# Weight-conversion halves of a fused attention and gated-layer kernel paced by 0.24 instead of 0.38 a unit, up to unit 21 instead of 24

## The chip, the cores and the metric

The kernel runs on one core of a Trainium2 chip. The metric is the device time of one execution in microseconds (us), as the median of several executions. A difference of over 0.2% (2.0 us here) is told apart from no change.

## What is computed

Causal attention with a decay (batch 4, 8 heads, 576 positions, head size 64), then a gated layer (512 to 1536 to 512), then a second layer (512 to 2048 to 512), all over 2304 tokens:

```
scores = scale * (q @ k^T) + cum[i] - cum[j], causal; attn = softmax(scores); x = attn @ v
x = (sigmoid(x @ w_gate) * (x @ w_val)) @ w_out
h = x @ w_in;  x = (h * clip(h + 3, 0, 6) / 6) @ w_out2
```

The five weights arrive as 64-bit floats and are used as pairs of 32-bit numbers (a high part and a rest).

## The kernel before

**Attention.** The 32 heads are taken as 16 pairs. Each pair has four **units** (row blocks of queries), so there are 64 units, numbered by `t`; pairs 0 to 6 take them in rising order, later pairs in falling order. For unit `t`, PE (TensorE) first turns the probabilities of unit `t - 3` (`tt`, L220; three units deep), then computes the scores of unit `t` (`st`, L216). DVE (VectorE) adds the decay and finds the row extreme (L500, two to four instructions a unit), ACT (ScalarE) takes the exponential (L508), DVE forms the reciprocal (L543, L544), POOL (GpSimd) normalises (L546). Scores have three PSUM banks and a unit uses two, so the scores of unit `t + 1` wait until the first L500 of unit `t` has read its bank. At the last unit of a pair PE also forms probabilities times values (`pv <- etA, etB`). Up to pair 6 PE turns q and k (`tq`, `tk`, `tl`, with DVE copies such as L415 and L426); from pair 7 on DVE turns them (L398, L399, L402).

**Filler.** From unit 23 on, one group of 12 matmuls of the gated layer is put into most units by `Filler.one` (L779): for each of three token chunks of 512, eight groups `pg` and `pv` (gate and value, four each) and then four groups `po` (output). The last unit of a pair has none. A group is only begun when its weights have been issued (`Gated.after`, L699); if they haven't, the unit goes without a group. Groups that are left when the attention ends run behind it, back to back.

**Conversion.** The weights of these groups are made in 12 **halves** (two each for gate 0, value 0, gate 1, value 1, output 0, output 1). A half loads 512 KB, takes three DVE instructions on 128x512 (L107, L108, L114) with one ACT instruction (L111) between the second and the third, then a high part (POOL L64 for halves issued before unit 16, ACT L62 from there on) and a rest (POOL L65). `Converter.run(n, engs)` (L183) adds `n` to an account at each unit from unit 4 on and issues a half for each full 1.0. A scheduler then places the instructions on each engine; each engine runs its own in that order.

Of the kernel before, what the change touches and what calls it, by code (L numbers as in the profile page):

```python
# [20 lines left out]
def attn_moe_kernel(  # L21
# [21 lines left out]
    NQ = 4  # L43
# [150 lines left out]
    conv = Converter()  # L194
# [856 lines left out]
    class Second:  # L1051
# [93 lines left out]
        def unit(self, k, x, ys, temps, between={}):  # L1145
            u1, u2, p5 = temps
            g, tt = self.ga[k % 2], nc.vector.tensor_tensor
            r11, r22, r12 = self.act(u1, g, 0, 0), self.act(p5, g, 1, 1), self.act(u2, g, 1, 0)
            r21 = self.act(x(), g, 0, 1)
            then = {1: (r11,), 2: (r11,), 3: (r11,), 4: (r22,), 5: (r12, r22, r22), 6: (r21, r12, r12, r21, r21)}  # L1150
            for s in range(7):
                if s in (1, 3):
                    y = ys.pop(0)()
                o = y if s % 2 else x()
                self.product(o, k, s, s in (0, 1, 3))
                if s in (0, 2, 3):
                    nc.scalar.copy({0: u1, 2: u2, 3: p5}[s], o)  # L1157
                elif s < 6:
                    c = {1: u1, 4: p5, 5: u2}[s]
                    tt(c, c, o, ALU.add)  # L1160
                for r in then.get(s, ()):
                    next(r)
                if k % NQ2 == NQ2 - 1:
                    self.load_block(k // NQ2 * 7 + 7 + s)
                if s in between:
                    between[s]()
# [72 lines left out]
    EA = (nc.scalar, nc.gpsimd, nc.gpsimd)  # L1239
    EF = (nc.scalar, nc.scalar, nc.gpsimd)  # L1240
    WU = (8, 4, 4, 4)

    KD, KT, RT = 4, 7, 0

    CA, C0, CB, CC = 0.65, 4, (1.8, 1.0, 1.5, 1.7, 2.0), 1.0

    CE, CS = 0.38, 0.12


    NGA, NCA, GA = 2, 3, 1  # L1250

    NSA = 8
# [111 lines left out]
    for t in range(len(units) + 3):  # L1364
        for job in (fixed, expo, norm, prep):
            job(t)
        if t == 2:
            eight = ep.tile([P, S], F32, tag="e", name="eight")[: B * H]
            nc.vector.tensor_scalar(eight, cum, -8.0, 1.0, ALU.mult, ALU.mult)
            nc.sync.dma_start(cum_d[1], eight)  # L1370
        p, s = unit(t - 4)
        if p and s == p.order[-1] and p.hp == NP - 1 and p.b < NCA:
            done = p.b + 1
        p, s = unit(t - 5)
        if p and s == p.order[-1] and t < len(units) + 3:
            fill.load(p.b, p.hp + 1)
        if t >= C0:
            conv.run(CS if len(conv.jobs) <= 2 * NSA - 6 * NGA else CE if t < NQ * (KT - 1) else CA, EA if t < NQ * KD else EF)
        fill.n = done
    att.close()  # L1380
    pace["dve"] = None
# [63 lines left out]
```

## Time and profile before

| what | value |
|---|---|
| median of 3 runs | 1002.28 us (1002.18 to 1002.36) |
| profiled execution, its own time | 1003.57 us |
| its span, first to last instruction | 1001.8 us |
| busy share of PE, DVE, ACT, POOL over the span | 98%, 53%, 48%, 29% |
| granted TensorE clock, mean | 0.998 of full speed |

The span is 1.77 us shorter than the profiled execution's own time, and that execution is 1.29 us above the median of the runs. Times inside the profile count from the start of the span. The attention ends at about 279 us; the two layers fill the rest.

### The profile page before, as it was taken

The numbers are of one execution on the slowest core, as the hardware profiler recorded it, in microseconds if no ns is written. First come the engines' busy times: TensorE is split into PE (matmuls) and PEld (weight loads), VectorE is DVE, ScalarE is ACT, GpSimd is POOL, SyncE is SP. The second block draws the span as 40 slices with busy tenths as digits, with TensorE's granted clock in tenths as the row PEclk, the third lists the DMA queues.
The fourth block names the chain that finished last, engine by engine and source line by source line (L and its number), as shares of the span: only waits on it lengthen the run. The fifth ranks groups of instructions, "written<-read, shape, count | busy, mean of one in ns | idle before, by whom it ended". The sixth has DMA issues, their size and how long they took to land.

```text
span 1001.8 us, 16150 instructions
## 1 busy us (share of the span) xinstructions
PE 986.5 (98%) x5733; PEld 810.4 (81%) x5733; DVE 530.9 (53%) x1220; ACT 476.9 (48%) x1094; POOL 290.5 (29%) x360
## 2 busy tenths in 40 slices
PE   8889999999999999999999999999999999999998
PEld 4556766667688889988888888899899898998987
DVE  6777856645347543737777574553534443333322
ACT  6787677667634432424434343453444443433322
POOL 3675655545323220302334131111111111111110
PEclk9999999999999999999999999999999999999999
DMA  7999796744324352566977578654686845753211
GB/s 184 294 250 226 198 244 156 185 143 145 119 79 154 117 166 82 175 210 264 331 258 252 179 270 318 245 198 166 237 330 206 293 147 193 294 209 148 81 66 64
DMA packets 141072, 197.30 MB, mean 197 GB/s; under 512 B 84192, under 2 KB 93408, under 8 KB 136896
## 3 DMA queue, kind: packets, MB, share of 16 engines
q1 hardware_dynamic: 140944, 196.20, 59.9%
q8 instruction: 45, 0.74, 0.3%
q14 instruction: 35, 0.29, 0.1%
q10 hardware_dynamic: 48, 0.07, 0.0%
HBM read 142.88 MB, written 53.36 MB: 196 GB/s over the span
## 4 chain that ended last, share of the span: by engine, by line
PE 91%; DVE 3%; ACT 2%; DMA 2%; issue 1%; POOL 0%; SPq 0%; DVEq 0%; ACTq 0%; POOLq 0%
PE po L216 34%; PE pv L216 18%; PE u L216 17%; PE pg L216 15%; PE st L216 4%; PE tt L220 3%; DVE e L500 1%; DMA kn<-in_k_dram 1%; ACT e L508 1%; DMA cum_d<-eight 1%; DMA x_d<-x 0%; DVE raw L108 0%; ACT raw L111 0%; ACT etB L580 0%; PE o L216 0%
## 5 line engine op out<-in xcount | busy, mean ns | idle before, releaser
L216 PE MATMUL po<-w,big 128*128 128x512 f32 x864 | 200.5, 390 | 0.0
L216 PEld LDWEIGHTS po<-w,big 128*128 128x128 f32 x864 | 161.8, 188 | 32.8
L216 PE MATMUL pg<-big,wg 128*128 128x512 f32 (+1 forms) x720 | 161.9, 371 | 0.0
L216 PE MATMUL pv<-big,wv 128*128 128x512 f32 (+1 forms) x720 | 161.4, 371 | 0.0
L216 PE MATMUL po<-big,wo 128*128 128x512 f32 (+1 forms) x720 | 160.9, 371 | 0.2 <-DVE big L65 0.2
L216 PEld LDWEIGHTS pg<-big,wg 128*128 128x128 f32 x720 | 125.8, 189 | 27.2 <-issue 4.0
L216 PEld LDWEIGHTS pv<-big,wv 128*128 128x128 f32 x720 | 125.6, 189 | 26.8 <-issue 4.5
L216 PEld LDWEIGHTS po<-big,wo 128*128 128x128 f32 x720 | 125.6, 189 | 25.7 <-issue 2.2
L1160 DVE TENSOR_TENSOR h<-h,u 128x384 f32<-128x384 f32 x69 | 38.2, 554 | 154.0 <-PE u L216 154.0
L546 POOL TENSOR_SCALAR e<-e,m 128x256 f32<-128x256 f32 (+4 forms) x144 | 86.8, 617 | 48.8 <-DVE m L544 32.1
L508 ACT ACTIVATE e<-e,m 128x256 f32<-128x256 f32 (+4 forms) x144 | 83.6, 584 | 31.6 <-DVE m L500 20.3
L216 PE MATMUL u<-h,big 128*128 128x384 f32 x504 | 90.2, 336 | 0.4 <-DVE h L1160 0.4
L216 PE MATMUL u<-h,h 128*128 128x384 f32 x504 | 90.1, 336 | 0.0
L216 PEld LDWEIGHTS u<-h,big 128*128 128x128 f32 x504 | 88.3, 188 | 1.8 <-DVE h L1160 0.8
L216 PEld LDWEIGHTS u<-h,h 128*128 128x128 f32 x504 | 88.4, 188 | 1.0
L1109 POOL TENSOR_TENSOR big<-tail,big 128x384 fp32r<-128x384 f32 x30 | 30.5, 1018 | 196.5 <-PE u L216 115.5
L1157 ACT COPY h<-u 128x384 f32<-128x384 f32 x69 | 32.8, 475 | 111.5 <-PE u L216 111.5
L500 DVE CUSTOM_DVE_ANT_0 e<-st,dc 128x384 f32<-128x384 f32 (+3 forms) x110 | 53.5, 520 | 47.9 <-PE st L216 30.3
L872 DVE SCALAR_TENSOR_TENSOR sg<-sg,pv 128x512 f32<-128x512 f32 (+1 forms) x48 | 29.7, 618 | 92.3 <-PE pv L216 59.7
L111 ACT ACTIVATE raw<-raw 128x512 f32<-128x512 f32 x68 | 45.6, 682 | 67.1 <-DVE raw L108 64.5
L62 ACT CAST big<-sg 128x512 fp32r<-128x512 f32 (+1 forms) x60 | 34.8, 580 | 60.6 <-DVE sg L872 54.6
L114 DVE SCALAR_TENSOR_TENSOR raw<-raw 128x512 int32<-128x512 int32 x68 | 52.5, 782 | 19.4 <-ACT raw L111 18.9
(141 smaller groups left out, 1202.8 us busy)
## 6 DMA issues: line engine op xcount, KB each, us to landing
h<-xc_d SPq DMA_DIRECT2D x21, 768.0 KB, 7.2
big<-x_d SPq DMA_DIRECT2D x28, 512.0 KB, 5.8
raw<-in_moe_w_out_dram SPq DMA_DIRECT2D x28, 512.0 KB, 3.7
h<-wt_d SPq DMA_DIRECT2D x12, 1024.0 KB, 7.4
big<-wt_d SPq DMA_DIRECT2D x12, 1024.0 KB, 7.6
x_d<-x SPq DMA_DIRECT2D x16, 576.0 KB, 3.9
h<-wb_d SPq DMA_DIRECT2D x12, 768.0 KB, 4.6
big<-wb_d SPq DMA_DIRECT2D x12, 768.0 KB, 5.2
```

Of the source, the lines that this page charges most:

```text
L62: nc.scalar.copy(hi, src)
L111: nc.scalar.activation(e, e, AF.Copy, scale=2.0**-112)
L114: nc.vector.scalar_tensor_tensor(low, high, 3, low, ALU.logical_shift_left, ALU.bitwise_or)
L216: i = nc.tensor.matmul(*a, **k)
L220: i = nc.tensor.transpose(*a)
L500: i = nc.vector.tensor_tensor_reduce(out=e, in0=st, in1=d, op0=ALU.add, op1=ALU.min, scale=self.by, scalar=init, accum_out=m[:, a : a + 1],)
L508: nc.scalar.activation(e, e, AF.Exp, bias=m[:, a : a + 1], scale=-1.0, accum_out=m[:, 4 + b : 5 + b])
L546: pace["pool"] = nc.gpsimd.tensor_scalar(e, e, m[:, 12 + j : 13 + j], 1.0, ALU.mult, ALU.mult)
L872: pace["dve"] = nc.vector.scalar_tensor_tensor(sg, sg, 1.0, pv, ALU.add, ALU.mult)
L1109: (nc.vector if f else nc.gpsimd).tensor_tensor(lo, sg, hi.bitcast(F32), ALU.subtract)
L1157: nc.scalar.copy({0: u1, 2: u2, 3: p5}[s], o)
L1160: tt(c, c, o, ALU.add)
```

## The change

The account gets 0.24 instead of 0.38 a unit, and the faster rate of 0.65 begins at unit 21 instead of unit 24 (`NQ * (KT - 1)`). The rate of 0.12 after the twelfth half stays.

```
-    CE, CS = 0.38, 0.12
+    CE, CS, CT = 0.24, 0.12, 21
...
-            conv.run(CS if len(conv.jobs) <= 2 * NSA - 6 * NGA else CE if t < NQ * (KT - 1) else CA, EA if t < NQ * KD else EF)
+            conv.run(CS if len(conv.jobs) <= 2 * NSA - 6 * NGA else CE if t < CT else CA, EA if t < NQ * KD else EF)
```

Worked through the account, the twelve halves are issued at these units:

```
before: 6  9 11 14 17 19 22 24 26 27 29 30
change: 8 12 16 20 22 23 25 27 28 30 31 33
```

On DVE, the first half, before (units 6 to 7 of pair 1; `raw` is the weight, `e` the scores with decay, `x` the attention's output):

```order
L544 RECIPROCAL m<-m 128x2
L107 TENSOR_SCALAR raw<-raw 128x512
L646 TENSOR_TENSOR x<-pv,x 128x256
L108 SCALAR_TENSOR_TENSOR raw<-raw 128x512
L114 SCALAR_TENSOR_TENSOR raw<-raw 128x512
L646 TENSOR_TENSOR x<-pv,x 128x320
L500 ISA e,m<-st,dt 128x288
```

and with the change (units 8 to 9 of pair 2):

```order
L415 TENSOR_SCALAR qp<-tq 128x512
L544 RECIPROCAL m<-m 128x1
L107 TENSOR_SCALAR raw<-raw 128x512
L108 SCALAR_TENSOR_TENSOR raw<-raw 128x512
L500 ISA e,m<-st,dc 128x384
L500 ISA m 128x1
L500 ISA e,m<-st,dc 128x384
L500 ISA m 128x1
L543 TENSOR_SCALAR m<-m 128x4
L426 COPY kp<-tk 128x512
L114 SCALAR_TENSOR_TENSOR raw<-raw 128x512
```

The whole half stood ahead of the last unit's L500 of a pair; now two of its instructions stand ahead of the second unit's L500 and the third behind it. The halves of units 12, 16 and 20 stand at the same place of pairs 3, 4 and 5.

On PE, units 32 to 34 before (`po` is an output group, `wo` its weights):

```order
L216 MATMUL st<-kp,qz_144 128x288 x2
L216 MATMUL po<-big,wo_1692 128x512 x6
L216 MATMUL po<-big,wo_1883 128x512 x6
L220 MATMUL tt<-ident,e 128x64 x12
L216 MATMUL st<-kp,qp 128x512 x2
L216 MATMUL po<-big,wo_1692 128x512 x6
L216 MATMUL po<-big,wo_1883 128x512 x6
L220 MATMUL tt<-ident,e 128x64 x12
L216 MATMUL st<-kp,qp 128x384 x2
```

and with the change:

```order
L216 MATMUL st<-kp,qz_144 128x288 x2
L220 MATMUL tt<-ident,e 128x64 x12
L216 MATMUL st<-kp,qp 128x512 x2
L220 MATMUL tt<-ident,e 128x64 x12
L216 MATMUL st<-kp,qp 128x384 x2
```

The twelfth half now comes at unit 33, so units 32 and 33 have no group; every later group stands two slots later, and three instead of one `po` groups are left for the end of the attention. Up to unit 31 the order on PE is the same in both.

On DVE, between units 31 and 32 before:

```order
L398 STREAM_TRANSPOSE qp<-qn 128x512
L399 STREAM_TRANSPOSE kp<-kn 128x576
L544 RECIPROCAL m<-m 128x2
L726 SCALAR_TENSOR_TENSOR sg<-sg,pv 128x512
L500 ISA e,m<-st,dt 128x288
```

and with the change:

```order
L398 STREAM_TRANSPOSE qp<-qn 128x512
L399 STREAM_TRANSPOSE kp<-kn 128x576
L544 RECIPROCAL m<-m 128x2
L107 TENSOR_SCALAR raw<-raw 128x512
L108 SCALAR_TENSOR_TENSOR raw<-raw 128x512
L726 SCALAR_TENSOR_TENSOR sg<-sg,pv 128x512
L114 SCALAR_TENSOR_TENSOR raw<-raw 128x512
L500 ISA e,m<-st,dt 128x288
```

The half of unit 31 now stands ahead of the first L500 of unit 32.

## Rows read from the trace of the kernel before

**Rows 1.** Page, part 1: busy us, share of the span, instructions.
```profile
PE 986.5 (98%) x5733; PEld 810.4 (81%) x5733; DVE 530.9 (53%) x1220; ACT 476.9 (48%) x1094; POOL 290.5 (29%) x360
```

**Rows 2.** Stretch table: length; busy PE, PEld, DVE, ACT, POOL; clock, DMA share, GB/s.
```profile
36.00:83.00 47.00, 41.27 (x425) 24.86 (x425) 38.10 (x138) 41.17 (x128) 34.80 (x50) 1.00 0.98 267
...
100.00:126.00 26.00, 26.00 (x209) 18.32 (x208) 21.80 (x61) 18.43 (x51) 16.93 (x20) 1.00 0.75 202
```

**Rows 3.** Timeline of PE, units 4 to 23: start, length, instruction, [idle before, releaser].
```profile
18.69 0.50 PE L216 MATMUL st<-masks,identb 128*128 128x384 bf16 x2
...
32.02 0.51 PE L216 MATMUL st<-masks,identb 128*128 128x384 bf16 x2 [2.06 <-DVE m L500]
...
44.46 0.50 PE L216 MATMUL st<-masks,identb 128*128 128x384 bf16 x2
...
48.18 0.29 PE L216 MATMUL st<-masks,identb 128*128 128x128 bf16 x2 [1.41 <-ACT raw L111]
...
58.19 0.50 PE L216 MATMUL st<-masks,identb 128*128 128x384 bf16 x2 [0.70 <-DVE m L500]
...
70.24 0.50 PE L216 MATMUL st<-masks,identb 128*128 128x384 bf16 x2 [0.20 <-DVE m L500]
...
73.64 0.29 PE L216 MATMUL st<-masks,identb 128*128 128x128 bf16 x2 [1.09 <-ACT raw L111]
...
82.95 0.27 PE L220 MATMUL tl<-ident,kn 128*128 128x128 f32 x1
```

**Rows 4.** Stretch table of PE around the idle at 32 us; clock behind the bracket.
```profile
33.00:34.00 1.00, 1.00 (x14) 0.50 1.20 191
...
36.00:37.00 1.00, 1.00 (x20) 1.00 1.01 249
```

**Rows 5.** Timeline of DVE: second unit of pair 2 and of pair 4.
```profile
37.46 0.56 DVE L500 CUSTOM_DVE_ANT_0 e<-st,dc 128x384 f32<-128x384 f32 x1 [0.65 <-PE st L216]
...
62.99 0.56 DVE L500 CUSTOM_DVE_ANT_0 e<-st,dc 128x384 f32<-128x384 f32 x1 [0.96 <-POOL dt L386]
```

**Rows 6.** Groups of DVE by shape, 20 to 83 us: busy us, mean ns, idle before.
```profile
L108 DVE SCALAR_TENSOR_TENSOR raw<-raw 128x512 int32<-128x512 int32 x7 | 5.9, 839 | 0.1
...
L114 DVE SCALAR_TENSOR_TENSOR raw<-raw 128x512 int32<-128x512 int32 x7 | 4.8, 692 | 2.2 <-ACT raw L111 2.2
...
L107 DVE TENSOR_SCALAR raw<-raw 128x512 int32<-128x512 int32 x7 | 2.9, 408 | 0.0
```

**Rows 7.** The same groups of DVE, 100 to 126 us.
```profile
L108 DVE SCALAR_TENSOR_TENSOR raw<-raw 128x512 int32<-128x512 int32 x4 | 3.9, 980 | 0.1
L114 DVE SCALAR_TENSOR_TENSOR raw<-raw 128x512 int32<-128x512 int32 x4 | 3.3, 824 | 1.6 <-ACT raw L111 1.4
L107 DVE TENSOR_SCALAR raw<-raw 128x512 int32<-128x512 int32 x4 | 2.8, 712 | 0.0
```

**Rows 8.** Timeline of PE, units 32 to 35.
```profile
126.03 2.80 PE L216 MATMUL po<-big,wo 128*128 128x512 f32 x10
...
129.74 0.59 PE L220 MATMUL tt<-ident,e 64*128 64x64 f32 x12
130.16 1.08 PE L216 MATMUL st<-kp,qp 64*128 64x512 f32 x4
131.17 3.06 PE L216 MATMUL po<-big,wo 128*128 128x512 f32 x12
134.15 0.58 PE L220 MATMUL tt<-ident,e 64*128 64x64 f32 x12
...
138.59 0.87 PE L216 MATMUL st<-kp,qp 64*128 64x128 f32 x8
```

**Rows 9.** Timeline of DVE between units 31 and 32.
```profile
125.64 0.70 DVE L398 STREAM_TRANSPOSE qp<-qn 128x512 f32<-128x512 f32 x1
...
127.55 0.45 DVE L500 CUSTOM_DVE_ANT_0 e<-st,dt 128x288 f32<-128x288 f32 x1
```

**Rows 10.** Chain that ended last, behind the attention: start, us, what.
```profile
289.78 2.72 PE pg L216 x12
```

## The prediction

> **What bounds the kernel now.** I read the page's first part, then the table of stretches, then the timelines of PE and DVE. PE is busy for 986.5 of 1001.8 us [rows 1]. The change takes no work from PE and gives it none, so the time can only move by what PE idles (15.3 us in all), by its clock, and by where it idles anew. From 100 us on PE shows no gaps: 26.00 of 26 us busy in the next stretch [rows 2]. Units 4 to 23, which have no groups of the gated layer, are where it waits: between 36 and 83 us PE is busy for 41.3 of 47 us, DVE for 38.1 and ACT for 41.2, and the DMA share is 0.98 [rows 2]. These are the units that the change relieves. What it pays with lies in units 27 to 35.
>
> **Early: what leaves.** Take the first mask matmuls of each pair as marks: 18.69, 32.02, 44.46, 58.19, 70.24 us, and the last flip of k before the first group, 82.95, plus 0.2 for its own length [rows 3]. Five pairs thus take 13.3, 12.4, 13.7, 12.1 and 12.9 us, 64.5 in all. The fourth has only four short waits, of about 0.2 each (the last is the 0.20 at 70.24), so PE's own work in a pair is 12.1 - 0.8 = 11.25 us. The other 8.2 us are waits and clock. Three big waits stand next to halves: 2.06 us at 32.02 (the half of unit 6 stands ahead of the last L500s of pair 1), 1.41 at 48.18 (unit 11) and 1.09 at 73.64 (unit 19); the 0.70 at 58.19 belongs to unit 14 [rows 3]. Behind the 2.06 the granted clock is 0.50, half speed (1.2 of 2.4 GHz), and back at 1.00 by 36 us [rows 4]; it is why the pair that begins there needs 12.4 us although it waits little, and is worth about 1.0.
>
> **Early: what comes instead.** Four halves now stand at one place of pairs 2 to 5: L107 and L108 ahead of the second unit's L500, L114 behind it. They take 0.41 + 0.84 = 1.25 us [rows 6]. DVE idles ahead of that L500 today for 0.65 us (pair 2) and 0.96 (pair 4) [rows 5]. So 0.3 to 0.6 shows; I take 0.5, since L108 is at times longer. L114 (0.69, rows 6) then delays the third unit's L500 by less than the values matmuls that follow on PE cover. A pair without a half gets 11.25 + 0.5 for its short waits, a pair with one 11.25 + 0.5 + 0.5 = 12.25. Pair 1 has none: 11.75. Pairs 2 to 5 have one each; pair 5 also has the one of unit 22, which is the place and unit of a half today, and its cost there, under the first group, is not new. The sum is 11.75 + 4 x 12.25 = 60.75 against 64.5: **-3.7 us**. Bounds: if all 1.25 shows in each of the four pairs, it is 11.75 + 4 x 13.0 = 63.75, a gain of 0.8 only; if all hides, 5 x 11.75 = 58.75, a gain of 5.7. A loss is left out, because today's fourth pair, with its half at unit 17, already runs in 12.1. The sixth half now comes at unit 23, not 24. Its 1.9 us on DVE stand beside the first group, which keeps PE busy for 2.7 [rows 10], so I price it at nothing; were that cover gone, it would cost its own 1.9.
>
> **Queues.** A half also brings one load of 512 KB on SP and, before unit 16, two POOL instructions. Two such loads leave the time before unit 21, where the DMA engines are full [rows 2]. The others are moved past loads of q, k and v by a few places; I put nothing on that, since the loads stand a pair ahead of their use. If it goes wrong it is inside the bounds.
>
> **Late: what is lost.** The output groups need all twelve halves. They come at unit 33 instead of 30, so units 32 and 33 lose their groups. Today these take 129.74 - 126.03 = 3.7 and 134.15 - 131.17 = 3.0 us [rows 8]. If the stretch became shorter by that 6.7, nothing would be lost: the two groups go to the end of the attention, where a group of 12 takes 2.72 [rows 10], together +5.44. The question is how much of the 6.7 PE gets back. Without the first `po`, PE reaches the scores of unit 33 at 126.03 + 0.6 = 126.6. They wait for the first L500 of unit 32, at 127.55 to 128.0 today [rows 9]. Now the three instructions of the half of unit 31 stand ahead of it: 1.9 us by the means before 83 us [rows 6], 2.5 by those after 100 us [rows 7]. That gives 129.9 to 130.5, less up to 0.8 because today's half of unit 29 is no longer ahead. I take 129.5; the scores stand at 130.16 today. So 0.6 of the first 3.7 comes back, and PE idles for 2.9 us. Unit 34 waits for POOL, which has the rest (L65) of that half ahead of the normalising, and then for the half of unit 33: I give back 1.0 of the second 3.0, the nearest to the first slot's share and less than half. An idle of 2.06 us lowered the clock [rows 3, 4], so 2.9 will, too: it cost 1.0 there, and I take 0.6 here, since PE has less to do. Returned: 0.6 + 1.0 - 0.6 = 1.0. **Net +4.4 us.** Bounds: nothing returned and the clock paid in full, 5.44 + 1.0 = +6.4; all returned, 5.44 - 6.7 = -1.3.
>
> Rows 6 and 7 differ: a half's three DVE instructions take 1.94 us in the window of units 5 to 22, and 2.52 in that of units 27 to 31. The Trainium skill (GPSIMD Engine Reference, section Specifications) says that POOL shares its SBUF interfaces with VectorE and that they contend when a VectorE instruction reads two SBUF inputs or runs in a two-port mode. By that rule the two more halves in units 27 to 33 cost DVE 5.0 us instead of 3.9, the late loss is 1.1 larger, and the time would be 1004.1. The trace agrees in sign, but it can't tell POOL's share from other causes.
>
> **Sum.** -3.7 + 4.4 = +0.7. On the profiled execution that is a span of 1002.5 and a time of 1004.3; the median stands 1.29 lower, so I say **1003.0 us**. A difference under 2.0 us (0.2%) is no change to a measurement.
>
> **Rivals.**
> - *The idle units pay nothing back* (slower). The L500 of unit 32 comes at 130.5 or later and PE works at half clock behind it. For it: five instead of three halves stand in units 27 to 33 of DVE's queue. Against it: DVE has one half less in unit 29. -3.7 + 6.4 = +2.7: 1005.0. It is slower by over 0.2% from a return below about -0.3 us.
> - *The early waits aren't the halves'* (slower). ACT, busy for 41 of 47 us [rows 2], or POOL sets the pace, and moved halves make new waits. For it: ACT's share. Against it: the fourth pair. -0.8 + 4.4 = +3.6: 1005.9.
> - *DVE has caught up by unit 32* (faster). The L500 of unit 32 comes by 127.5, PE idles little, the clock stays. For it: DVE's waits for scores in units 27 to 29, since PE is the slower there. Against it: the new order puts the half right ahead. With 5.0 of 6.7 returned, -3.7 + 0.4 = -3.3: 999.0. It takes a return of over 3.7 to be told from no change.
> - *The change isn't what it says.* By the order it is, for places; but six halves, not four, are issued by the first group's unit 23. That is in the sum.
>
> **Chances.** Forecast (between -2 and +2) 0.55; first rival 0.18, second 0.10, third 0.17. So slower 0.28, same 0.55, faster 0.17. The range from 1000.2 to 1005.9 takes in the first two rivals' times and leaves out most of the third and the tails.
>
> **What would show it.** In the profile after: the 2.06 at 32 us and the half clock behind it gone, and pairs 2 to 5 at 12.0 to 12.5 us each, right or wrong for the early part. An idle of PE of 2 to 4 us ahead of unit 33's scores, released by DVE L500, and a lower clock behind it, for the late part; three `po` groups behind the attention. Unit 23's first group should start 3 to 4 us earlier, and the attention end within 2 us of today plus the two groups. I am wrong if the first group starts less than 2 us earlier, or if the scores of unit 35, which start at 138.59 today [rows 8], move ahead by the early gain and most of the 6.7 us besides.

## The result and the profile after

The change made the kernel slower: 1010.75 us median of 6 runs (1010.32 to 1013.24) against 1002.32 us (1001.17 to 1005.44) for the kernel before, measured with it. The ratio is 1.0084, with a 95% interval from 1.0066 to 1.0103. The forecast was 1003.0 us with a range up to 1005.9, so the loss of 8.4 us lies outside it. The profiled span is 1011.0 us against 1001.8.

Page, part 1, of the kernel after (busy us, share, instructions), against [rows 1]:

```profile
PE 989.4 (98%) x5733; PEld 811.5 (80%) x5733; DVE 534.8 (53%) x1220; ACT 477.6 (47%) x1096; POOL 284.3 (28%) x358
```

PE runs the same 5733 matmuls and is busy 2.9 us longer, which fits the half-speed stretches below; so 6.3 of the 9.2 us of span are idle time of PE. The stretch table of the kernel after (columns as in [rows 2]):

```profile
36.00:83.00 47.00, 41.45 (x409) 25.24 (x409) 37.05 (x132) 39.74 (x121) 28.31 (x45) 1.00 0.92 245
92.00:96.00 4.00, 4.00 (x15) 2.45 (x12) 2.31 (x8) 2.38 (x6) 3.42 (x6) 0.57 0.90 202
134.00:138.00 4.00, 2.44 (x16) 1.37 (x16) 1.95 (x6) 2.28 (x7) 3.80 (x7) 0.50 0.60 106
```

In the first stretch DVE, ACT and POOL have less to do than before and the DMA share is 0.92, not 0.98 [rows 2]. The mean granted clock is 0.57 in the second and 0.50 in the third: half speed (1.2 of 2.4 GHz) for most or all of it.

Timeline of PE in the kernel after, units 4 to 27 (start, length, instruction, [idle before, releaser]), against [rows 3]:

```profile
19.12 0.50 PE L216 MATMUL st<-masks,identb 128*128 128x384 bf16 x2
...
30.47 0.50 PE L216 MATMUL st<-masks,identb 128*128 128x384 bf16 x2
...
36.54 0.28 PE L216 MATMUL st<-masks,identb 128*128 128x128 bf16 x2 [1.28 <-DVE m L500]
...
80.63 2.31 PE L216 MATMUL pg<-big,wg 128*128 128x512 f32 x9
83.64 0.97 PE L216 MATMUL pg<-big,wg 128*128 128x512 f32 x3 [0.69 <-DMA big<-x_d]
...
90.98 0.46 PE L220 MATMUL tt<-ident,e 64*128 64x64 f32 x8 [1.69 <-POOL e L546]
...
105.09 1.24 PE L216 MATMUL st<-kp,qz 128*128 128x288 f32 x4
```

The waits at 32.02, 48.18 and 73.64 of [rows 3] are gone. Each pair with a half (marks at 30.47, 42.92, 55.60 and 68.27) has a new one of 1.28 to 1.33 us ahead of the second unit's second mask matmul, as at 36.54. The first group starts at 80.63 us, 2.35 earlier than before, and then waits for the last quarter of x. The flips of unit 22 wait 1.69 us for POOL.

Timeline of PE in the kernel after, units 31 to 35, against [rows 8]:

```profile
122.41 0.87 PE L216 MATMUL st<-kp,qp 64*128 64x128 f32 x8
...
131.63 0.59 PE L220 MATMUL tt<-ident,e 64*128 64x64 f32 x12 [3.58 <-ACT etB L580]
132.02 1.14 PE L216 MATMUL st<-kp,qp 64*128 64x512 f32 x4
134.84 0.37 PE L220 MATMUL tt<-ident,e 64*128 64x64 f32 x2 [1.68 <-ACT e L508]
...
142.37 0.87 PE L216 MATMUL st<-kp,qp 64*128 64x128 f32 x8
```

The two `po` groups are gone from this stretch, and it is longer all the same: from the scores of unit 31 (122.41) to those of unit 35 (142.37) it takes 19.96 us. Before, it took 138.59 - 120.78 = 17.81. Timeline of PE before, scores of units 27 and 31:

```profile
103.55 1.24 PE L216 MATMUL st<-kp,qz 128*128 128x288 f32 x4
...
120.78 0.88 PE L216 MATMUL st<-kp,qp 64*128 64x128 f32 x8
```

The two lost `po` groups run behind the attention now, where a group takes 2.72 [rows 10]. From the scores of unit 35 to the end it takes 1011.0 - 142.37 = 868.6 us, and took 1001.8 - 138.59 = 863.2.

Starts on PE in us, from the timelines of the profiled executions, in the order in which the kernels appear below:

| kernel | unit 4, first mark | first group | scores of unit 27 | of unit 31 | of unit 35 | span |
|---|---|---|---|---|---|---|
| before | 18.69 | 82.98 | 103.55 | 120.78 | 138.59 | 1001.8 |
| after | 19.12 | 80.63 | 105.09 | 122.41 | 142.37 | 1011.0 |
| late_only | 19.20 | 81.44 | 102.80 | 120.03 | 133.58 | 1002.6 |
| place1 | 18.98 | 76.01 | 102.55 | 119.88 | 140.50 | 1009.2 |
| late_crowd | 19.28 | 82.12 | 102.90 | 120.12 | 141.19 | 1010.1 |
| a_spread | 19.21 | 80.71 | 106.42 | 123.65 | 139.92 | 1009.3 |

### The profile page after: what moved, and what is told of

It reads as the page before. It is cut to its first block, busy times and chain, and to the rows that moved or that the text cites. A ratio compares the mean times of both kernels' runs of the same rounds, so it can differ in the third digit from the quotient of the medians.

```text
span 1011.0 us, 16147 instructions
## 1 busy us (share of the span) xinstructions
PE 989.4 (98%) x5733; PEld 811.5 (80%) x5733; DVE 534.8 (53%) x1220; ACT 477.6 (47%) x1096; POOL 284.3 (28%) x358
## 4 chain that ended last, share of the span: by engine, by line
PE 93%; DVE 3%; issue 2%; ACT 1%; POOL 1%; DMA 0%; DVEq 0%; POOLq 0%; ACTq 0%
PE po L216 34%; PE pv L216 19%; PE u L216 17%; PE pg L216 14%; PE st L216 5%; PE tt L220 3%; DVE e L500 1%; PE o L216 1%; POOL e L546 0%; DVE raw L107 0%; DVE qp L415 0%; DMA vn<-in_v_dram 0%; DVE xp L890 0%; DVE raw L108 0%; PE tk L220 0%
## 5 line engine op out<-in xcount | busy, mean ns | idle before, releaser
L546 POOL TENSOR_SCALAR e<-e,m 128x256 f32<-128x256 f32 (+4 forms) x144 | 83.3, 592 | 49.7 <-DVE m L544 39.0
L508 ACT ACTIVATE e<-e,m 128x256 f32<-128x256 f32 (+4 forms) x144 | 83.4, 583 | 27.8 <-DVE m L500 15.9
L111 ACT ACTIVATE raw<-raw 128x512 f32<-128x512 f32 x68 | 45.4, 677 | 67.3 <-DVE raw L108 63.6
L500 DVE CUSTOM_DVE_ANT_0 e<-st,dc 128x384 f32<-128x384 f32 (+3 forms) x110 | 53.4, 520 | 43.8 <-PE st L216 27.1
L62 ACT CAST big<-sg 128x512 fp32r<-128x512 f32 (+1 forms) x60 | 34.8, 580 | 58.3 <-DVE sg L872 55.4
```

The lines of the kernel that those rows point to most:

```text
L62: nc.scalar.copy(hi, src)
L111: nc.scalar.activation(e, e, AF.Copy, scale=2.0**-112)
L500: i = nc.vector.tensor_tensor_reduce(out=e, in0=st, in1=d, op0=ALU.add, op1=ALU.min, scale=self.by, scalar=init, accum_out=m[:, a : a + 1],)
L508: nc.scalar.activation(e, e, AF.Exp, bias=m[:, a : a + 1], scale=-1.0, accum_out=m[:, 4 + b : 5 + b])
L546: pace["pool"] = nc.gpsimd.tensor_scalar(e, e, m[:, 12 + j : 13 + j], 1.0, ALU.mult, ALU.mult)
```

## The experiments

In all of them a half is issued at listed units in place of the account, so that the places can be chosen one by one:

```
-    CE, CS = 0.38, 0.12
+    HU = (6, 9, 11, 14, 17, 19, 22, 24, 26, 27, 29, 30, 38, 46, 54, 63)
...
-            conv.run(CS if ... else CE if ... else CA, EA if t < NQ * KD else EF)
+            conv.run(1.0 if t in HU else 0.0, EA if t < NQ * KD else EF)
```

This list has the units of the kernel before; `(8, 12, 16, 20, 22, 23, 25, 27, 28, 30, 31, 33, 37, 46, 54, 62)` those of the change. Only the twelve first numbers are named below. The theory behind the first runs (A) adds up three pieces, one for each place where the table above shows a loss or gain; the rival (B) is that the two lost groups are the loss.

**late_only.** The early part of before, and only the twelfth half moved, from 30 to 33.

> Edit: the halves of the kernel before, at the same units, but the twelfth at unit 33 instead of 30; units 32 and 33 lose their groups, nothing early changes. Theory A (three pieces add up: early -2.8 us, units 23 to 26 +4.3, units 32 to 35 +2.1, two groups behind the attention +5.4): the tail's 5.4 stays, and PE gets back 1 to 4 of the 6.7 us of units 32 and 33, since the half of unit 31 is not ahead of unit 32's scores: 1004 to 1007 us. Theory B (the lost slots alone make the loss; the rest is noise of the loads): 1009 to 1011 us.

Measured 1003.99 us, ratio 1.0015 [1.0005, 1.0024]. Timeline of PE in this kernel, units 31 to 35:

```profile
120.03 0.87 PE L216 MATMUL st<-kp,qp 64*128 64x128 f32 x8
...
126.38 0.59 PE L220 MATMUL tt<-ident,e 64*128 64x64 f32 x12 [0.72 <-ACT etB L580]
...
128.80 0.93 PE L220 MATMUL tt<-ident,e 64*128 64x64 f32 x12 [0.91 <-ACT etB L580]
...
133.58 0.88 PE L216 MATMUL st<-kp,qp 64*128 64x128 f32 x8
```

13.55 us for the stretch: 4.26 of the 6.7 us of groups come back, and with 5.8 us more behind unit 35 the loss is small. B falls: losing two groups is not what costs 8 us. A's time, 1004 to 1007, holds only at its lower edge.

**early_only.** The change's early part, and its late halves brought forward so that no group is lost: 8, 12, 16, 20, 22, 23, 25, 27, 28, 29, 30, 31.

> Edit: the early halves of the change (units 8, 12, 16, 20, 22, 23, 25, 27, 28) and the last three at 29, 30, 31, so that no group loses its unit. Theory A: -2.8 + 4.3 = +1.5 by unit 27, nothing or a little in units 27 to 32: 1003 to 1006 us, with an idle of PE of 1.5 to 2 us ahead of the flips of unit 22. Theory B: 1000 to 1002.5 us.

Measured 1011.42 us, ratio 1.0095 [1.0080, 1.0110]: as slow as the change, against both. Timeline of PE in this kernel, unit 32:

```profile
134.35 0.54 PE L216 MATMUL po<-big,wo 128*128 128x512 f32 x1 [2.98 <-ACT wo L62]
```

The groups are kept, but the first `po` stops in its middle for its own weights, whose conversion is at the same late units. So it is as slow without a lost group as the change is with two.

**a_dz.** The change, with POOL's masked copy of the decay (`hide`, L449) issued behind the normalising:

```
-        if s > 1:
-            p.hide(s - 1)
-        if s == 2:
-            p.hide(0)
+        with behind(pace["pool"]):
+            if s > 1:
+                p.hide(s - 1)
+            if s == 2:
+                p.hide(0)
```

> Edit: the changed kernel, and the mask instructions on the decay (L449) put behind the last normalising instead of where the scheduler found room, so POOL's queue does not stand behind the load of pair 7's decay. Theory A: the idle of 1.7 us ahead of the flips of unit 22 and the half clock behind it go: 1006 to 1008 us. Theory B: 1010 to 1011 us.

Measured 1012.75 us, ratio 1.0095 [1.0077, 1.0113]. POOL's wait at unit 22 is gone, but the first group now waits 3.45 us for x, and unit 27 starts at 105.26, as in the change. Both theories' times missed.

**place1.** The change, with its first four halves one unit later: 9, 13, 17, 21.

> Edit: the changed kernel with its first four halves one unit later (9, 13, 17, 21), that is ahead of the third unit's L500 of a pair instead of the second's. Theory A: each exposes about 0.2 us of PE idle instead of 1.3, so the first group starts 4 us earlier (at about 76.5 us); but POOL still stands behind the load of pair 7's decay, which lands no earlier, so most of it is lost again by unit 26: 1008.5 to 1011 us. Theory B: what is gained early stays: 1006 to 1007 us.

Measured 1008.67 us, ratio 1.0066 [1.0049, 1.0082]. Timeline of PE in this kernel, unit 23:

```profile
82.13 1.65 PE L216 MATMUL pg<-big,wg 128*128 128x512 f32 x3 [3.80 <-DMA big<-x_d]
```

None of the waits of 1.3 us is left (0.25 at most), and the first group starts at 76.01, 4.6 us earlier than in the change. Then it waits 3.80 us for x, and by unit 27 only 2.5 us are left of the lead. A's time held and the early gain does end at a load, but at that of x: no flip waits for POOL up to unit 27.

**late_crowd.** The early part of before, the late halves of the change: 6, 9, 11, 14, 17, 19, 22, 25, 28, 30, 31, 33.

> The early part of the kernel before (first seven halves where they were), and the last five halves at units 25, 28, 30, 31 and 33, close together as in the change; two groups lost. Theory A (the five halves crowded into units 27 to 33 stand in the queues of VectorE, ScalarE and POOL ahead of what the flips wait for): scores of unit 31 to unit 35 take 19 to 20.5 us as in the change (20.0), with flips idle 2 to 4 us behind etB, where the kernel that lost the same two groups with its halves apart took 13.55; time 1008 to 1011. Theory B (the late loss is carried over from the units before, which started late and at half clock): with the old early part the stretch takes 13 to 15 us and the time is 1003 to 1005.

Measured 1009.99 us, ratio 1.0064 [1.0040, 1.0088]. Timeline of PE in this kernel, units 31 to 35:

```profile
120.12 0.87 PE L216 MATMUL st<-kp,qp 64*128 64x128 f32 x8
...
128.97 0.59 PE L220 MATMUL tt<-ident,e 64*128 64x64 f32 x12 [3.21 <-ACT etB L580]
...
132.18 1.41 PE L220 MATMUL tt<-ident,e 64*128 64x64 f32 x8 [1.28 <-POOL e L546]
...
141.19 0.87 PE L216 MATMUL st<-kp,qp 64*128 64x128 f32 x8
```

A held but for the stretch, which at 21.07 us is over its 20.5, behind an early part that is as good as before. (The count in the expectation was loose: four of the halves lie in units 27 to 33 here, five in the change.) So the late halves alone lose 6.8 us (1003.23 for the kernel before in this series) of the change's 8.4.

**a_spread.** The change's early part, then 25, 26, 27, 29, 30, 33.

> The change with its early part, and its last halves one unit or two earlier: units 25, 26, 27, 29, 30 and 33 and not 25, 27, 28, 30, 31 and 33; the same two groups lost. Theory A (the late loss is the crowd of five halves in units 27 to 33): with four in these units the flips of unit 34 no longer wait 3.6 us behind etB, scores of unit 31 to unit 35 take 13.5 to 16 us instead of 20.0, time 1005 to 1008. Theory B (the late loss comes from the early part's lateness): the stretch stays at 18.5 us or more, time 1009.5 to 1012.

Measured 1009.65 us, ratio 1.0066 [1.0053, 1.0079]. The stretch takes 16.27 us, just above A's 16, and well under B's 18.5. The flips ahead of unit 33's scores (the expectation calls them those of unit 34) still wait 3.00 us for `etB`, against A, but the waits behind them are gone. The time missed A's range because the first group waited 3.17 us for x here (0.69 in the change), so unit 27 started 1.3 us later than there. Four halves lie in units 27 to 33, as in late_crowd; they come one unit earlier, at 27, 29 and 30 instead of 28, 30 and 31, and the stretch is 4.8 us shorter (3.7 against the change, which has the same early part). So with the count kept the place makes a difference; that the count costs nothing is not shown, since late_only, with three, takes 13.55.

**What the halves of units 30 and 31 do.** Timelines of ACT and of DVE in the kernel after:

```profile
129.86 0.67 ACT L111 ACTIVATE raw<-raw 128x512 f32<-128x512 f32 x1 [2.41 <-DVE raw L108]
130.43 1.06 ACT L580 COPY etB<-tt 128x512 f32<-128x512 f32 x2
```

```profile
131.17 0.45 DVE L500 CUSTOM_DVE_ANT_0 e<-st,dt 128x288 f32<-128x288 f32 x1
```

ACT runs in order. The half's L111 stands ahead of the evictions `etB` of the flips, and waits 2.41 us for DVE's L108 of the same half, which stands behind two turns of q and k (L398, L399). PE's flips of unit 30, ahead of unit 33's scores, wait for these evictions: the 3.58 us at 131.63. The scores behind them also need the L500, which ends at 131.62. But L111 is not all of it: in a_spread no half is issued at unit 31, and the flips wait 3.00 us. Timelines of PE and of ACT in a_spread:

```profile
132.28 0.59 PE L220 MATMUL tt<-ident,e 64*128 64x64 f32 x12 [3.00 <-ACT etB L580]
```

```profile
130.55 0.62 ACT L62 CAST big<-sg 128x512 fp32r<-128x512 f32 x1 [1.12 <-DVE sg L726]
131.08 1.06 ACT L580 COPY etB<-tt 128x512 f32<-128x512 f32 x2
```

Here `etB` stands behind an eviction of the gated layer (L62), which waits for DVE's L726 behind the same two turns. Five kernels side by side, from the timelines: the end of these evictions counted from the start of unit 31's scores, the two halves of the stretch, and PE's mean granted clock from 130 to 134, 134 to 138 and 138 to 142 us:

| kernel | halves at 30, 31 | end of `etB` | scores of 31 to 33 | of 33 to 35 | clock |
|---|---|---|---|---|---|
| before | 30 | 8.47 | 9.38 | 8.43 | 1.00, 1.00, 1.00 |
| late_only | neither | 6.21 | 6.74 | 6.81 | 1.00, 1.00, 1.00 |
| a_spread | 30 | 8.49 | 9.03 | 7.24 | 0.85, 0.72, 1.00 |
| after | both | 9.08 | 9.61 | 10.35 | 0.87, 0.50, 0.77 |
| late_crowd | both | 8.70 | 9.25 | 11.82 | 0.50, 0.50, 0.73 |

The evictions were as late before as in a_spread. There PE had the `po` group of unit 32 to run meanwhile; without the group the same lateness is idle time. Against before, late_only moves nothing up to there but the half of unit 30, and its evictions come 2.3 us earlier. The half of unit 31 adds up to 0.6 us to the evictions and 3.1 to 4.6 us to the second part (after and late_crowd against a_spread, whose other late halves differ, too). Timeline of POOL in the kernel after:

```profile
132.63 1.80 POOL L65 TENSOR_TENSOR wo<-raw,wo 128x512 fp32r<-128x512 f32 x1 [2.36 <-ACT wo L62]
134.41 2.30 POOL L546 TENSOR_SCALAR e<-e,m 128x128 f32<-128x128 f32 x4
```

The rest of the half of unit 31 (L65) stands ahead of the normalising of unit 31, whose flips PE runs ahead of unit 34's scores. The profile puts the wait of 1.68 us there down to ACT's L508, the same wait in late_crowd (1.28) to POOL's L546.

**a_xact, a_st, a_st_ldp, b4_st_ldp: x's store and load on other engines.** The result of the fourth pair goes to DRAM (`x_d<-x`, L650) and comes back as the last quarter of x (`big<-x_d`, L205). Four kernels moved one or both of these, nothing else: in a_xact the load goes to ScalarE, in a_st the store, in a_st_ldp the store to ScalarE and the load to POOL, and b4_st_ldp does the same to best4_dz, below.

```
-        nc.sync.dma_start(
+        (nc.scalar if ring["x"] == 4 else nc.sync).dma_start(
             x.bitcast(F32), src[:, kc * P : (kc + 1) * P, t0 : t0 + T]...
...
-            nc.sync.dma_start(x_d[:, rows, cols]...
+            (nc.scalar if self.i == 3 else nc.sync).dma_start(x_d[:, rows, cols]...
```

> The change, with the load of the fourth quarter of x (the one that the first group of the gated layer waits for) issued by ScalarE and no longer by SP behind two loads of keys; all else in order as in the change. Theory A1 (the load's place in SP's queue caps units 23 to 26): the first group no longer waits for x, the load lands 1.5 to 2 us earlier, scores of unit 27 start at 102.5 to 104 (105.1 in the change), time 1008.5 to 1010. Theory A2 (the DMA engines are full, or the store of x just lands late, so no place in a queue helps): it lands within 0.7 us of the change's 83.6, unit 27 within 0.7 us of 105.1, time 1010 to 1012.

> The change, with one store moved from SP's queue to ScalarE's: the fourth pair's result, which stood ready at 67.4 us and was stored at 71.97, behind loads on SP. The load that reads it back stays on SP. Theory S (SP's queue is late, but the load's own place behind two loads of keys is the bound): the store goes at 68 to 69, the load at 77.5 to 79.4, the first group waits 0 to 0.7 us for it, POOL still waits for the decay; 1009 to 1011.5. Theory T (the store's lateness alone is the bound): the load goes 3 us or more earlier and the time is 1006 to 1008.

> As the run before this one, and the load that reads this result back is issued by POOL, in a place where POOL stood idle for 2.45 us. Theory S (SP's queue, its order and its backlog, is what holds x back, and not the DMA engines): x lands before 80 us and the first group doesn't wait; SP has two entries fewer, so the decay lands up to 1 us earlier; scores of unit 27 start at 102.5 to 104.5 (105.1 in the change); time 1007.5 to 1010. Theory D (the DMA engines are full, so an earlier issue doesn't help): x lands after 82 us.

> The same kernel with only the fourth pair's store on ScalarE and its load back on POOL. Theory S: the wait of 0.97 for x at unit 23 goes, scores of unit 27 start 0.5 to 1.5 us earlier (100.3 there), time 1000.5 to 1002. Theory D: x lands no earlier than 82 us, time as there, 1002 to 1003.

Measured 1016.37, 1013.67, 1017.56 and 1008.36 us. As times these runs are useless: each made the issuing engine wait, and that cost more than the question was worth. As probes they are good. Timeline of ACT in a_xact:

```profile
78.94 1.07 ACT L580 COPY etB<-tt 128x512 f32<-128x512 f32 x2 [5.30 <-DMA x_d<-x]
```

ACT waited for the store to land before it issued the load at 78.45: SP issued the store at 71.14 us, and it landed 7.2 us later, with no place in SP's queue between. So the store that lands late, one of A2's reasons, is what this row shows; unit 27 started at 108.51, against both theories. Timeline of ACT in a_st:

```profile
70.50 0.40 ACTq L650 DMA_DIRECT2D x_d<-x  x1
70.94 0.21 ACT L436 COPY kp<-tl 128x64 f32<-128x64 f32 x1 [3.27 <-DMA big<-x_d]
```

The result was ready at about 67 us (at 67.42 in the change, by DVE's L646), and the store was not issued before 70.50, 4.75 us after the load of the third quarter (65.75): the issue waited for that load. It is not a matter of their data. In the trace of the change each of the program's 510 transfers, from the ninth on, tells its landing by the same semaphore as the one eight places before it, and none is issued before that one has landed. The load of the third quarter (issued at 66.39, landed 5.2 us later) stands eight places ahead of the store (71.97).

In a_st_ldp the load was issued at 67.86 and the store at 72.84 (4.98 later), in b4_st_ldp at 64.66 and 69.70 (5.04). In a_st S and T both fell: the store does not only stand behind loads, it waits for one. In the other two POOL issued the load back at 80.36 and 77.52, and the times missed the ranges given.

**a_wide, b_wide.** The change and the kernel before, with the loads of q and k in blocks (L352) reading rows of 2304 bytes instead of pieces of 128 bytes. Count, order and bytes stay; q and k hold other elements.

```
-                    t[32 * g : 32 * g + 32].rearrange("r (t c) -> r t c", c=32),
-                    src[..., :, g % 2 * 32 : g % 2 * 32 + 32].rearrange("(t r) c -> r t c", r=32),
+                    t[32 * g : 32 * g + 32],
+                    src[..., g % 2 * 288 : g % 2 * 288 + 288].rearrange("(r t) c -> r (t c)", r=32),
```

> The change, with the loads of q and k in blocks (four each, 32 rows of 18 pieces of 128 bytes) reading as many bytes in rows of 2304 bytes; order, count and bytes of all loads stay, q and k hold other elements. Theory D (the DMA engines' time, taken up by short packets, holds back x and the decay): the fourth pair's x lands before 82 us, the first group waits less than 0.3 us and the flips of unit 22 less than 0.8; scores of unit 27 start at 101 to 103 (105.1 in the change), so 1006 to 1009. Theory Q (SP's order alone, with each entry waiting for the one eight places before, sets the times): x lands within 0.7 us of the change's 83.6, unit 27 within 1 us of 105.1, 1009.5 to 1012.

> The same edit to the kernel before. Theory D: there the first group doesn't wait for x and POOL's wait for the decay costs 0.64 at unit 22, so little is to be won: 1000.5 to 1003, and the loss by the change shrinks from 8.4 us to 5 to 7 between these two runs. Theory Q: as the kernel before within 1 us, and the loss by the change stays at 8 us or more.

Measured 1010.28 us, ratio 1.0083 [1.0066, 1.0100], and 1001.83 us, ratio 0.9990 [0.9980, 1.0000]. Timeline of PE in a_wide, unit 25:

```profile
89.73 0.46 PE L220 MATMUL tt<-ident,e 64*128 64x64 f32 x8 [1.10 <-POOL e L546]
```

D held in part: the first group (80.89) doesn't wait for x and unit 27 starts at 102.30 us, 2.8 earlier than in the change; but x landed at 83.0 and not before 82, and the flips waited 1.10 us (D said under 0.8). The decay landed at 86.9 instead of 88.5, and the clock stayed at 1.00 from 92 to 96 us, where the change has 0.57. Q's times and x's landing held. The late stretch took 21.50 us here, so the lead was lost again, and the loss by the change stays 8.45 us between these two runs. So the shorter time of the loads of q and k is worth 2.8 us at unit 27, but that is not where the 8.4 us are made.

**Versions.** With a half where place1 had found it cheap, five variants looked for a kernel that beats both: best1 (5, 9, 13, 17, 21, 22, 24, 26, 27, 29, 30, 31), best1_dz (the same with the edit of a_dz), best4_dz (5, 9, 13, 17, 19, 21, 22, 24, 26, 27, 29, 30 with that edit), best5_dz (its last halves at 24, 25, 26, 28, 29) and b_dz (the kernel before with that edit). b4_sta is best4_dz with all stores of x on ScalarE.

> All early halves where a half was cheap: units 5, 9, 13, 17, 21 (ahead of the third unit's additions), then 22, 24, 26, 27, 29, 30, 31, so twelve by unit 31, no group lost. Theory A: no wait of 1.3 us behind VectorE's additions; the first group starts at 76 to 77.5 but waits for x till 82, so scores of unit 27 start at 101.5 to 103 (103.55 before); the seven halves of units 22 to 31 cost 1 to 3 us more than before up to unit 35; time 1000.5 to 1004. Theory B (only the number of early halves matters, their place does not): as before within 0.5 us up to unit 27, time 1002 to 1003.

> The kernel of the run before this one, with POOL's masked copy of the decay put behind the normalising of the unit. Theory A: POOL no longer stands 1 to 2 us behind the decay's load while flips of unit 22 wait, but the load of x keeps the cap, so the time is within 1 us of the run before. Theory B (POOL's wait for the decay was a bound of its own): 1.5 to 3 us faster than the run before.

> The kernel before, with POOL's masked copy of the decay put behind the normalising of the unit; the halves stay where they were. If POOL's wait for the decay's load is a bound of its own in the kernel before too, its flips of unit 22 (which wait 0.64 there) lose that wait: 0.5 to 1 us faster, 1001 to 1002. The rival (another order of POOL makes a later unit wait): 1003 or more.

> Halves at units 5, 9, 13, 17, 19, 21, 22 (seven by the first gated unit, each where a half was cheap), then 24, 26, 27, 29, 30 as in the kernel before; POOL's masked copy behind the normalising. Theory A (three bounds: the place of the early halves, POOL's wait for the decay, and halves too late for the groups that use them): scores of unit 27 start at 96.5 to 99 (103.55 before), no group waits for its own weights, and units 27 to 35 take what they took before (35.0), so 995 to 999. Theory B (what is won early is lost again behind loads further on): 1001 to 1005.

> As the run before this one, with the last halves at 24, 25, 26, 28 and 29, one unit earlier from the second on. Theory A: if groups still waited for their weights in the run before this one, 1 to 3 us faster than that; if none did, equal within 1 us, or slower by the crowd in units 24 to 26. Theory B: 1001 to 1005, as for the run before.

> The kernel with seven early halves in cheap places and POOL's masked copy moved (the one that came out 1 us faster than the kernel before), with all pairs' results stored by ScalarE and not by SP. Theory S: SP's queue is shorter by eight entries, loads land earlier, no wait of 0.97 for x at unit 23; 0.5 to 2 us faster than that kernel, 1000 to 1002. Theory D: within 0.5 us of it or slower, since ScalarE pays for the issues.

| kernel | median us | ratio, 95% interval | unit 27 | unit 35 |
|---|---|---|---|---|
| best1 | 1009.04 | 1.0052 [1.0035, 1.0069] | 103.41 | 145.06 |
| best1_dz | 1006.95 | 1.0043 [1.0027, 1.0059] | 96.78 | 137.91 |
| b_dz | 1004.29 | 1.0013 [1.0004, 1.0022] | 101.45 | 137.63 |
| best4_dz | 1002.28 | 0.9990 [0.9981, 0.9998] | 100.31 | 136.51 |
| best5_dz | 1003.56 | 1.0003 [0.9993, 1.0014] | 99.08 | 137.37 |
| b4_sta | 1005.10 | 1.0015 [0.9999, 1.0031] | 103.43 | 139.60 |

best1 missed both of its theories. best1_dz has unit 27 6.8 us earlier than the kernel before, and has lost nearly all of it by unit 35: its last halves come at 30 and 31, and the first `po` waits 3.56 us for its own weights, as in early_only. Against best1 it is 2.1 us faster in the median, as its theory B said, but the runs overlap (1004.0 to 1011.0 and 1004.3 to 1011.4), and the 6.6 us at unit 27 lie between its fastest execution and one of best1's slower ones. b_dz (1004.29) came out as its rival said, and a_dz no faster than the change, so it is not shown that POOL's place behind the decay's load is a bound of its own. best4_dz is the only one of these below the kernel before, by 1.0 us, less than the 2.0 that are told apart from no change; theory B (1001 to 1005) held, where A had put it at 995 to 999. Its first group starts at 79.32 us and waits 0.97 for x, and the first `po` waits 0.79 and 0.50 for ACT and DVE to write its input `big` (0.23 before), so 1.2 of the lead of 3.2 us at unit 27 is gone by unit 35. best5_dz held its theory B, b4_sta its theory D.

## Why the prediction was wrong

**Early, 3.7 us: 1.3 to 2.1 of it was one execution's accident.** The step "what leaves" took the 2.06 us at 32.02 and the half clock behind it [rows 3, 4] as the price of the half of unit 6. Four more profiled kernels have the same early halves, and at this mark they wait 0.70 (late_only), 1.34 (late_crowd), 1.49 (b_dz) and 0.98 us (b_wide), with the clock at 1.00 behind it; late_only and late_crowd differ from the kernel before at unit 24 at the earliest, and the mark is unit 8's. Timeline of PE in late_crowd:

```profile
31.88 0.50 PE L216 MATMUL st<-masks,identb 128*128 128x384 bf16 x2 [1.34 <-DVE m L500]
```

From the first mark to the first group the four take 62.2 to 63.0 us, and the five kernels with the change's early halves 61.5 to 61.6. The gain is 0.7 to 1.5 us. The 2.8 us between the two profiles (64.3 against 61.5) holds the accident, 1.3 to 2.1 us.

**Early, the price of a half: 0.5 was too small.** The pair without a half took 11.35 us (forecast 11.75), those with one 12.45, 12.68 and 12.67 (forecast 12.25). So a half costs 1.1 to 1.3 us against the pair without one, the upper bound of 1.25 rather than 0.5. What differs is the neighbour. Timelines of DVE and of POOL in the kernel after, pair 2:

```profile
34.19 0.68 DVE L107 TENSOR_SCALAR raw<-raw 128x512 int32<-128x512 int32 x1
34.90 1.11 DVE L108 SCALAR_TENSOR_TENSOR raw<-raw 128x512 int32<-128x512 int32 x1
```

```profile
33.19 1.39 POOL L386 TENSOR_SCALAR_AFFINE_SELECT dt<-dc 64x576 f32<-64x576 f32 x2
34.67 0.79 POOL L546 TENSOR_SCALAR e<-e,m 128x576 f32<-128x576 f32 x1
```

L107 and L108 take 1.79 us here, not the 0.41 + 0.84 of [rows 6], while POOL masks the decay (L386) and normalises the last unit of the pair (L546). All four halves are alike: 0.60 to 0.72 and 1.11. One unit later, in place1, the timeline of DVE shows

```profile
36.38 0.40 DVE L107 TENSOR_SCALAR raw<-raw 128x512 int32<-128x512 int32 x1
36.81 0.76 DVE L108 SCALAR_TENSOR_TENSOR raw<-raw 128x512 int32<-128x512 int32 x1
```

and 0.40 to 0.41 and 0.74 to 0.76 for its halves from 36 us on. So the means of [rows 6] held for other places. Over the 20 profiles, up to 150 us, L107 and L108 take 0.41 and 0.69 us in the median where POOL does nothing, and 1.08 and 1.70 where it runs L65 throughout. The Trainium skill (GPSIMD Engine Reference, section Specifications) says that POOL shares its SBUF interfaces with VectorE; the trace agrees that the same two DVE instructions are 0.6 us longer beside POOL's L386 and L546, and place1 takes the waits away by moving them.

**"Queues ... I put nothing on that": this step failed.** From the first group to unit 27 the kernel before takes 20.57 us, the change 24.46, a loss of 3.9 us that no term of the sum held (late_only and late_crowd, with the early halves of before, take 21.36 and 20.78). Timelines of POOL in the kernel after and before:

```profile
88.59 0.41 POOL L449 TENSOR_SCALAR_AFFINE_SELECT dz<-dc 128x256 f32<-128x256 f32 x1 [7.92 <-DMA dc<-cum_d]
88.97 1.29 POOL L65 TENSOR_TENSOR wg<-raw,wg 128x512 fp32r<-128x512 f32 x1
90.23 1.36 POOL L546 TENSOR_SCALAR e<-e,m 128x512 f32<-128x512 f32 x2
```

```profile
87.99 0.41 POOL L449 TENSOR_SCALAR_AFFINE_SELECT dz<-dc 128x256 f32<-128x256 f32 x1 [6.09 <-DVE m L500]
```

POOL stood 7.92 us for the decay; the conversion's L65 follows, then the normalising (L546), and the flips run from 90.98. With the 0.69 for x and the 0.20 at the next flips these waits are 2.6 us, 1.9 more than the 0.64 that the flips waited before. Behind them the clock is 0.57 for 4 us, which makes 1.7 us more (0.43 x 4). But the decay landed hardly later than before. In the change it was issued at 80.98 and took 7.5 us, so it landed at 88.5; before, it was issued at 82.28 and took 5.7, so it landed at 88.0, and POOL's L449 began at 87.99 (the profile puts that wait down to L500). PE came 2.35 us earlier to a transfer that lands 0.5 us later, so with POOL in this order the early gain ended there, as it ended at x in place1. The last quarter of x landed at 83.6 instead of 81.8. Timelines of SP around the fourth pair's store, before and after:

```profile
71.72 0.55 SPq L650 DMA_DIRECT2D x_d<-x  x1
72.36 0.42 SPq L101 DMA_DIRECT2D raw<-in_moe_w_val_dram  x1
...
76.93 0.99 SPq L205 DMA_DIRECT2D big<-x_d  x1
```

```profile
68.53 0.39 SPq L101 DMA_DIRECT2D raw<-in_moe_w_gate_dram  x1
...
71.97 0.55 SPq L650 DMA_DIRECT2D x_d<-x  x1
...
77.47 1.80 SPq L352 DMA_DIRECT2D kn<-in_k_dram  x2
79.38 0.44 SPq L205 DMA_DIRECT2D big<-x_d  x1
```

Before, the half's load of 512 KB stands behind the store of x, and now ahead of it. By the profile's list of transfers the store landed 4.5 us after its issue before and 6.8 us after it in the change, and the load back then stands behind two loads of k. In the other kernels whose store SP issues, it took 6.0 to 8.9 us where the half's load stands ahead (five kernels) and 3.9 to 5.5 us where it stands behind (eight), but 6.7 us in place1, where it also stands behind. So the place of that load goes with a late store, and is not shown to be its only cause. Why the decay took 1.8 us longer stays open: there the half's load stood ahead before and stands behind in the change. The forecast asked only whether the loads that moved were late for their own use; they weren't (no L107 of the change waits for its load up to 96 us). What the transfers would hold back, and that PE would reach them earlier, it did not ask.

**Sixth half at unit 23, priced at nothing.** No run took this half alone, so this step stays open.

**Late, the tail: right.** The two lost groups were put at 5.44 us behind the attention; from unit 35 to the end it is 5.4 us more in the change, 5.8 in late_only and 5.7 in late_crowd.

**Late, what returns: the first slot nearly, the second not at all.** The forecast was 1.0 us of 6.7; measured is -2.15 (19.96 against 17.81). From unit 31 to 33 it takes 9.61 us against 9.38 before, where 0.6 was to come back. The step had the right size of idle (2.9 forecast, 3.58 measured), and its L500 did come late: it ended at 131.62, 3.6 us later than before, 1.6 of that because unit 31 started later. It missed that the evictions `etB` were late even before, and that the lost group had covered this; they ended at 131.49, next to the L500. From unit 33 to 35 it takes 10.35 us against 8.43: "I give back 1.0 of the second 3.0" became -1.9. The step named what stood in the way, L65 on POOL, and priced it too low: flips wait 1.68, 0.33 and 0.30 us. It also priced the clock too low, at 0.6. From 133 to 139 us the clock is 0.50 and PE is busy for 3.6 us, from 139 to 140 it is 0.60; half of the 3.6 and 0.4 make 2.2 us, an estimate. Against late_only, whose flips wait 0.91 us there at full clock, the longer waits and the clock make 3.6 us, and 10.35 - 6.81 is 3.5. The first rival (nothing returned, half clock) is nearest to this, but its 6.4 us for the late part were still under the 7.6 measured (2.15 + 5.44).

**Sum.** By the two profiles: 0.43 later at unit 4, then -2.78, +3.89, +0.09 up to unit 31, +2.15, and +5.4 behind unit 35: 9.2 us. The forecast's sum held the second, the fifth and the sixth, with -3.7, -1.0 and +5.44. The largest error is the term that wasn't there (3.9 us), the next the late stretch (1.0 + 2.15 = 3.2), the third the early gain (0.9 by the two profiles, 2.2 to 3.0 by the other eight executions).

## What to carry to other kernels

Price an instruction at a new place by rows of that place, with what its neighbours on other engines do at that moment, and follow a moved step through the in-order queue of each engine that it touches: here the rest of a conversion on POOL stood ahead of the normalising that PE's flips needed. When work is taken out of a slot, look what it covered: here evictions that were as late before. Count transfers by what they may hold back, and ask of an early gain which transfer it will run into. And before a wait in one profile is booked as a gain, look whether a second execution of the same order shows it.

## What the runs showed that was not expected

The fourth pair's store of 576 KB landed 3.9 us (b_wide) to 8.9 us (a_wide) after its issue. The same order on the engines gave medians from 1001.93 to 1003.47 us for the kernel before in the separate series, and single executions up to 1008.09; waits of 0.7 to 2.1 us at one mark are part of that. The granted clock fell to half behind idles of PE of 1.69 + 0.20 us (unit 25) and 3.58 us (unit 33) in the change, and stayed at 1.00 behind 1.18 + 0.20 us at the same flips in late_only.
